# One order table for another: an attention-plus-gate kernel with its instruction order, engine choices, PSUM banks and filler matmuls replaced

## The chip, the cores and the metric

The kernel runs on one core of a Trainium2 chip. A core has five engines that run side by side and meet only through semaphores: TensorE (PE, matrix products into PSUM), VectorE (DVE), ScalarE (ACT), GpSimd (POOL) and SyncE (SP, which here only issues transfers). The metric is the device time of one execution in microseconds (us); less is better.

## The reference

Eight batches of eight heads, 576 rows, head size 64. Queries and keys pass through a feature map, the attention is linear, and its output goes into a gated linear unit with a causal convolution of five taps.

```python
def phi(x):
    proj = np.einsum('bhsd,df->bhsf', x, w_phi)              # f = 128
    proj = proj - np.max(np.abs(proj), axis=-1, keepdims=True)
    return np.concatenate([np.exp(proj), np.exp(-proj)], axis=-1)
q_p, k_p = phi(q), phi(k)
kv  = np.einsum('bhsf,bhsd->bhfd', k_p, v);  z = np.sum(k_p, axis=2)
num = np.einsum('bhsf,bhfd->bhsd', q_p, kv)
den = np.einsum('bhsf,bhf->bhs', q_p, z)[..., None] + 1e-06
x = (num / den)   # heads joined: [8, 576, 512]
gate = 1 / (1 + np.exp(-causal_conv5(x, conv_w)))            # per channel
return (gate * (x @ w_val)) @ w_out
```

## The kernel before

The work is cut into 1062 small tasks, and every task belongs to one engine (or to the transfer engines). `build` makes them in the same way in both kernels: for each of the eight batches, and for five units of up to four 128-column blocks each, it makes

- **loads**: batch 0's keys and queries come as float32 in nine pieces on SP's queue (`load32`, L525 and L527; four pieces of k, five of q) and are transposed on PE (`tp32`, L536) and copied to bf16 (`tc32`, L542 on DVE, L544 on ACT). From batch 1 on they are loaded and cast on POOL's queue (`load`, L550). Values come through `loadv` (L531): on POOL's queue for batch 1, on SP's for the others.
- **hold**: a one-column copy on POOL (`hold`, L509) that reads the last piece of batch 0's q. Since an engine works through its list in order, it keeps what stands behind it on POOL, the loads of batches 1 and 2, from being issued before that piece has landed.
- **keys**: projection on PE (`kp`, L577), maxima on DVE (`kmax`, L585), two exponentials per unit on ACT (`kexp`, L595), the row scale (`ek`, L604), v times that scale on POOL (`vs`, L610), and the product of keys and values (`st`, L620; its copy `kv`, L628/L632).
- **queries**: projection (`qm`, L577), maxima (`qmax`, L585), the maxima spread on POOL (`rx`, L682), projection less maxima (`qp`, L693/L698), exponentials (`qexp`, L706/L709).
- **output of the attention**: `num` (L719/L726), division on DVE (`nrm`, L737/L740), then the transpose into XT, on PE with a copy (`xtp`, `xtc`) or, in batches 6 and 7, by a transposing transfer issued from SP (`xtd`, L755).
- **gated unit**: `gate` (L781) with `tanh` (L785), `val` (L791) with `gv` (L797), `out` (L813, and L817 for the leftover rows of two batches), the copy out of PSUM (`oev`, L630 on DVE, L634 on ACT) and the store (`odma`, L830/L836).

Nothing schedules these at run time. `ORDER` is a table of task numbers: it is the order in which instructions are emitted, so each engine's list is the subsequence of its own tasks. `FLEX` says, for the 93 tasks that more than one engine can do, which engine does it (A, D or P). `BANKS` gives each group of tasks its PSUM bank or pair of banks. `WARM` and `ZERO` put extra matmuls on PE ahead of given places of the order: `warm` (L491) is one 512-column product whose result nobody reads, `zero` (L497/L504) adds zero products to a bank that a real task has just filled, so that whoever reads that bank waits for them too. Dependencies between engines become semaphore waits by themselves.

The loop that emits everything:

```python
for i, t in enumerate(plan.follow()):
    for _ in range(zero[i][1] if i in zero else 0):
        em.zero(plan.tasks[zero[i][0]])
    for _ in range(warm[i][1] if i in warm else 0):
        em.warm(warm[i][0])
    if t.fn is not None:
        t.fn(t)
```

## Time and profile before

| what | value |
|---|---|
| median of 3 runs | 219.54 us (218.94, 219.54, 221.03) |
| profiled execution, span from first to last instruction | 217.7 us |
| what lies around the span, by the median | 1.8 us |
| PE busy in the span | 195.5 us (90%), 3946 matmuls |
| ACT busy | 180.8 us (83%) |
| DVE busy | 170.2 us (78%) |
| POOL busy | 132.8 us (61%) |
| first exponential on ACT | at 9.21 us |
| last matmul over | at 212.52 us |

The profile gives the span of the one execution that it recorded and no whole time for it, so the median less the span stands for what lies around it. In the views quoted below, a row of the timeline begins with start and length in us, then engine and line, then what is written from what is read, and in brackets how long the engine stood idle ahead of it and who ended that. In a table of stretches the columns are length, busy time of PE, of its weight loads, of DVE, ACT and POOL (with the number of instructions), the granted PE clock, the share of the transfer engines and GB/s. A row of groups has its busy time, the mean duration in ns and the idle time ahead. A row of waits has the total, the number and the longest.

### The profile page before, as it was taken

Reading aid. Unit: us, or ns where it says so; the run is one execution under the profiler, and the core shown is the slowest. Engines: PE = TensorE matmul, PEld = TensorE weight load, DVE = VectorE, ACT = ScalarE, POOL = GpSimd, SP = SyncE. Lnnn points to the kernel's source line nnn. Section 1 sums busy time; section 2 is a strip of 40 time slices with the busy share of each in tenths; the row PEclk is TensorE's granted clock in tenths of the full one; section 3 lists DMA queues with packets and bytes.
Section 4 is the critical chain, followed back from the end, with each engine's and each line's share of the span. In section 5 each row is a group of like instructions: output and inputs, shape, how many; then the busy total and the mean of one; then the engine's idle time right before and its main releaser. Section 6 shows DMA issues by size and latency. Waiting matters only on the chain.

```text
span 217.7 us, 9029 instructions
## 1 busy us (share of the span) xinstructions
PE 195.5 (90%) x3946; PEld 138.6 (64%) x3946; DVE 170.2 (78%) x257; ACT 180.8 (83%) x267; POOL 132.8 (61%) x172
## 2 busy tenths in 40 slices
PE   2787887778999999998999999999999999899990
PEld 2555565566676676676857776567757766687740
DVE  3199979999789988997899978998699897654510
ACT  3589999999989899998999997999988988634251
POOL 3055999897793838970999089902993879210010
PEclk9999999999999999999999999999999999999997
DMA  6999998899899799989999778969953265764166
GB/s 177 364 234 215 302 188 231 149 174 199 144 152 284 139 135 213 302 154 174 233 276 168 88 165 248 190 142 203 287 183 89 63 160 128 81 168 97 48 186 202
DMA packets 49954, 39.92 MB, mean 183 GB/s; under 512 B 34165, under 2 KB 39541, under 8 KB 49914
## 3 DMA queue, kind: packets, MB, share of 16 engines
q1 hardware_dynamic: 43616, 28.65, 55.6%
q0 software_dynamic: 6032, 10.49, 26.3%
q8 instruction: 31, 0.51, 0.9%
q10 hardware_dynamic: 266, 0.21, 0.3%
q14 instruction: 9, 0.07, 0.1%
HBM read 30.48 MB, written 9.44 MB: 183 GB/s over the span
## 4 chain that ended last, share of the span: by engine, by line
PE 52%; ACT 23%; DVE 14%; DMA 5%; issue 4%; SPq 0%; DVEq 0%; ACTq 0%
PE PS L791 11%; ACT QTIL L706 9%; PE PS L781 9%; PE PS L813 9%; ACT KTIL L595 8%; DVE MQP L585 5%; PE PS L620 5%; PE PS L577 4%; PE PS L719 4%; DVE MK L585 3%; DMA KTIL<-in_k_dram 3%; PE PS L693 2%; DMA XT<-XN 2%; PE PS L817 2%; PE PS L698 2%
## 5 line engine op out<-in xcount | busy, mean ns | idle before, releaser
L595 ACT ACTIVATE KTIL<-PS 128x1024 bf16<-128x1024 f32 (+1 forms) x80 | 71.9, 960 | 4.1 <-PE PS L577 2.0
L610 POOL TENSOR_TENSOR VT<-VN,EK 128x1152 bf16<-128x1152 f32 x32 | 67.9, 2123 | 4.0 <-ACT EK L604 3.9
L706 ACT ACTIVATE QTIL<-PS 128x1024 bf16<-128x1024 f32 x64 | 62.5, 1044 | 2.4 <-PE PS L698 1.6
L682 POOL TENSOR_TENSOR RX<-MQR,ident 128x512 bf16<-128x512 bf16 (+1 forms) x39 | 36.6, 964 | 35.7 <-DVE MQR L670 26.0
L585 DVE TENSOR_REDUCE MK<-PS 128x8 f32<-128x1024 f32 (+1 forms) x40 | 44.2, 1112 | 2.9 <-PE PS L577 1.2
L585 DVE TENSOR_REDUCE MQP<-PS 128x8 bf16<-128x1024 f32 (+1 forms) x40 | 43.6, 1112 | 3.1 <-PE PS L577 2.3
L791 PE MATMUL PS<-XT,WV 128*128 128x288 bf16 x256 | 34.8, 286 | 0.3 <-DVE GV L797 0.2
L797 DVE SCALAR_TENSOR_TENSOR GV<-TH,PS 128x576 bf16<-128x576 bf16 x32 | 23.8, 752 | 10.4 <-PE PS L791 4.7
L813 PE MATMUL PS<-WOUT,GV 128*128 128x512 bf16 x128 | 31.3, 380 | 0.0
L791 PEld LDWEIGHTS <-WV 128*128 128x128 bf16 x256 | 23.8, 98 | 7.9 <-issue 1.4
L785 ACT ACTIVATE TH<-PS 128x576 bf16<-128x576 f32 x32 | 20.3, 663 | 9.5 <-PE PS L781 6.3
L620 PE MATMUL PS<-VT,KTIL 64*128 64x65 bf16 x1152 | 23.3, 191 | 1.1 <-issue 1.0
L781 PE MATMUL PS<-XT,GW 64*64 64x288 bf16 x640 | 23.1, 285 | 0.9 <-DMA XT<-XN 0.8
L740 DVE TENSOR_TENSOR XN<-PS,RCP 128x512 bf16<-128x512 f32 x32 | 22.1, 692 | 1.5 <-DMA XT<-XN 0.4
L620 PEld LDWEIGHTS <-KTIL 64*128 64x128 bf16 x1152 | 20.8, 94 | 3.8 <-issue 2.5
L719 PEld LDWEIGHTS <-QTIL 128*128 128x128 bf16 x512 | 18.3, 97 | 6.4 <-issue 4.0
L719 PE MATMUL PS<-KV,QTIL 128*128 128x65 bf16 x512 | 20.3, 194 | 0.3 <-DVE MQP L585 0.2
L781 PEld LDWEIGHTS <-GW 64*64 64x64 bf16 x640 | 17.8, 106 | 3.3 <-DVE RCP L737 0.9
L634 ACT ACTIVATE OUTS<-PS 128x512 f32<-128x512 f32 x22 | 13.5, 619 | 7.3 <-PE PS L813 6.1
L577 PE MATMUL PS<-W,qT 64*128 64x128 bf16 x288 | 15.1, 217 | 3.7 <-ACT qT L544 0.9
L813 PEld LDWEIGHTS <-GV 128*128 128x128 bf16 x128 | 11.1, 98 | 11.3 <-issue 0.6
L577 PEld LDWEIGHTS <-qT 64*128 64x128 bf16 x288 | 10.6, 94 | 10.3 <-issue 5.2
(79 smaller groups left out, 235.6 us busy)
## 6 DMA issues: line engine op xcount, KB each, us to landing
out_dram<-OUTS SPq DMA_DIRECT2D x32, 256.0 KB, 3.4
VN<-in_v_dram SPq DMA_DIRECT2D x7, 1152.0 KB, 6.3
KQN<-in_q_dram POOLq DMA_DIRECT2D x6, 576.0 KB, 8.3
KQN<-in_k_dram POOLq DMA_DIRECT2D x6, 576.0 KB, 9.8
KTIL<-in_k_dram SPq DMA_DIRECT2D x4, 288.0 KB, 4.5
VN<-in_v_dram POOLq DMA_DIRECT2D x1, 1152.0 KB, 10.6
KTIL<-in_q_dram SPq DMA_DIRECT2D x4, 256.0 KB, 5.7
out_dram<-OUTS SPq DMA_DIRECT2D x14, 64.0 KB, 2.6
```

The lines of the kernel that those rows point to most:

```text
L577: nc.tensor.matmul(self.PS[:, t.grp.banks[par], i * P:(i + 1) * P], X[rows, (c0 + i) * P:(c0 + i + 1) * P], self.W2[rows, :], start=True, ...
L585: self.nc.vector.tensor_reduce(o, self.two(t.grp, n * P).rearrange("p a (c f) -> p a c f", f=F), AX.X, ALU.max, apply_absolute_value=True)
L595: self.nc.scalar.activation(self.KTIL[b % 2][:, s, c0:c0 + n, :, :].rearrange("p c a f -> p a c f"), self.two(t.grp, n * P).rearrange("p a ...
L610: nc.gpsimd.tensor_tensor(self.VT[g][:, s, :, 0:D], self.VN[b % 2][:, NC * g:NC * g + NC, :], e.to_broadcast([P, NC, D]), ALU.mult)
L620: nc.tensor.matmul(self.PS[:, t.grp.banks[ab], (s * 2 + x) * E1:(s * 2 + x + 1) * E1], self.KTIL[b % 2][rows, s, J // 2, J % 2, :], self.V ...
L682: self.nc.gpsimd.tensor_tensor(o, *wide(self.MQR[self.mq(b, u)][:, :], self.ident2), ALU.mult)
L706: self.nc.scalar.activation(o, i, AF.Exp, scale=1.0 - 2.0 * s)
L719: nc.tensor.matmul(self.PS[:, t.grp.banks[h // 4], (h % 4) * E1:(h % 4 + 1) * E1], Q[:, s, c % 2, h, (c // 2) * P:(c // 2 + 1) * P], self. ...
L781: self.nc.tensor.matmul(self.PS[o * D:(o + 1) * D, t.grp.banks[par], 0:R], self.GW[r, jj, 4 - m, :], X[r, 4 * a + jj, :, HALO - 8 * s:HALO ...
L791: self.nc.tensor.matmul(self.PS[:, t.grp.banks[par], 0:R], self.WV[:, i, (2 * j + par) * D:(2 * j + par + 2) * D], X[:, 4 * par + i, :, HA ...
L797: nc.vector.scalar_tensor_tensor(out=self.GV[b % 3][:, j, :, :], in0=self.TH[j][:, :, :], scalar=1.0, in1=self.two(t.grp, R), op0=ALU.add, ...
L813: nc.tensor.matmul(self.PS[:, t.grp.banks[0], :], GV[:, j, c % 2, (c // 2) * XH:(c // 2) * XH + P], self.WOUT[:, j, c % 2, :], start=(j == ...
```

## The change

The functions are the same, line for line; five tables differ. The two tables at the top are shorter by two lines, so a line of the kernel before has a number smaller by 2 in the changed one (L595 becomes L593).

- `ORDER` holds the same 1062 tasks in another order. From about the 50th PE task on most tasks move by only a few places on their engine.
- `FLEX`: 21 tasks change engine. Twelve pass from ACT to DVE and eight from DVE to ACT; one spreading of maxima (`rx` of batch 0, unit 4) goes from DVE to POOL.
- `BANKS`: other PSUM banks for a number of groups.
- `ZERO`: 41 calls at 14 places become 10 calls at 3 places, 152 matmuls become 40. `WARM`: five places and six matmuls become four places and six matmuls.

```diff
-WARM = (
-    "60:6:1 81:1:1 87:7:2 134:7:1 141:7:1 "
-)
-ZERO = "35:76:7 61:80:5 75:34:1 101:105:1 118:99:1 126:215:8 144:223:1 155:192:4 158:200:1 175:315:6 189:346:1 195:241:2 197:241:2 211:327:1"
+WARM = "71:7:1 74:1:2 123:0:2 143:7:1"
+ZERO = "82:78:5 202:311:3 249:342:2"
...
-    "1 2 9 3 4 11 5 6 10 21 22 19 20 13 12 46 25 26 7 8 23 24 14 27 28 42 29 32 30 33 44 49 76 31 15 43 45 47 16 158 159 48 "
...
+    "1 2 3 4 27 28 7 8 21 22 19 20 5 9 6 25 182 26 23 24 40 11 183 29 10 158 41 159 160 42 12 161 301 44 46 302 32 47 45 30 "
...
-    "AAAAAADAAADDPPPPDDDDAADDDDDDDDDDDDDAAADAAAADDDDAAADDDAADAAADDADAADDDDADDDDADDDDDDAADADDAAAAAA"
+    "AAAADADAAADDPPPPPDDAAADDDDDDDDDDDDDDAADAADDDAADAAADDDAADADADDDDAADDDAADDADADADDADADADDDDADADD"
```

**The first loads, on SP.** KTIL1 here is the tile whose space first holds batch 0's float32 k and q, and VN0 holds values. SP's list began

```order
L527 DMA KTIL1_73<-in_k_dram 128x576 x3
L525 DMA KTIL1_73<-in_q_dram 128x512 x3
L527 DMA KTIL1_73<-in_k_dram 128x576
L525 DMA KTIL1_73<-in_q_dram 128x512
L525 DMA KTIL1_73<-in_q_dram 128x256
L531 DMA VN0_66<-in_v_dram 128x4x576
```

and now begins

```order
L525 DMA KTIL1_73<-in_k_dram 128x576 x2
L523 DMA KTIL1_73<-in_q_dram 128x256
L525 DMA KTIL1_73<-in_k_dram 128x576
L523 DMA KTIL1_73<-in_q_dram 128x512 x2
L525 DMA KTIL1_73<-in_k_dram 128x576
L523 DMA KTIL1_73<-in_q_dram 128x512 x2
L529 DMA VN0_66<-in_v_dram 128x4x576
```

The small last piece of q, the one that the hold reads, goes from ninth to third place, the third piece of k from third to seventh; the first full pieces of q come one place later.

**The first loads, on POOL.** After its memsets POOL's list went on with the hold, four loads (QTIL1 is batch 1's q and k, KQN are batch 2's), two spreadings of maxima (RX) and only then batch 1's values (VN1):

```order
L509 CAST HOLD_76<-KTIL1_73 128x1
L550 DMA QTIL1_75<-in_q_dram 128x2304
L550 DMA QTIL1_75<-in_k_dram 128x4x576
L550 DMA KQN1_65<-in_q_dram 128x2304
L550 DMA KQN0_64<-in_k_dram 128x4x576
L682 TENSOR_TENSOR RX1_135<-MQR0_90,ident2_130 128x512
L682 TENSOR_TENSOR RX0_134<-MQR0_90,ident2_130 128x512
L531 DMA VN1_67<-in_v_dram 128x4x576
L610 TENSOR_TENSOR VT0_82<-VN0_66,EK_86 128x18x64
```

and now

```order
L529 DMA VN1_67<-in_v_dram 128x4x576
L507 CAST HOLD_76<-KTIL1_73 128x1
L548 DMA QTIL1_75<-in_q_dram 128x2304
L548 DMA QTIL1_75<-in_k_dram 128x4x576
L548 DMA KQN1_65<-in_q_dram 128x2304
L680 TENSOR_TENSOR RX0_134<-MQR0_90,ident2_130 128x512
L680 TENSOR_TENSOR RX1_135<-MQR0_90,ident2_130 128x512
L457 DMA WV_139<-in_moe_w_val_dram 128x4x512
L548 DMA KQN0_64<-in_k_dram 128x4x576
L608 TENSOR_TENSOR VT0_82<-VN0_66,EK_86 128x18x64
```

Batch 1's values now stand ahead of the hold, batch 2's k stands behind the two spreadings, and the weights of `val` (WV) come right behind those spreadings, where they stood much further down.

**The first copies and exponentials, on ACT.** The casts are copies of transposed k (kT0) and q (qT0), the activations are exponentials of keys. Before:

```order
L544 CAST kT0_68<-PS_63 128x512 x3
L595 ACTIVATE KTIL0_72<-PS_63 128x2x4x128 x2
L544 CAST qT0_70<-PS_63 128x512
L595 ACTIVATE KTIL0_72<-PS_63 128x2x4x128
L544 CAST kT0_68<-PS_63 128x512
```

Now:

```order
L542 CAST kT0_68<-PS_63 128x512 x2
L593 ACTIVATE KTIL0_72<-PS_63 128x2x4x128 x3
L542 CAST qT0_70<-PS_63 128x512
L593 ACTIVATE KTIL0_72<-PS_63 128x2x4x128
L542 CAST kT0_68<-PS_63 128x512
```

The third copy of k leaves the head of the list, on PE the third transpose does the same, and the projections of the first two units follow the two transposes at once.

**The end.** On PE `num` of batch 6, chunk 0, stood behind two `st` of batch 7 and `qp` of batch 7's unit 2; it now follows `num` of chunk 1 directly, and those three tasks come after it. The last tasks on PE were seven `out` of batches 6 and 7 and, at the very end, the leftover rows (L817); now the leftover rows come fourth from the end and `out` of batch 7, chunk 0, is last.

10 lines of the change are left out of this document (5 added, 5 removed), and 70 rows, old and new, of the table ORDER.

## The prediction, on record before the changed kernel ran

> **What bounds the kernel now.** I read the page's busy shares first, then the table of stretches, then the timeline of the first 22 us and the chain that ended last. Shares and six of the stretches (length, busy PE, weight loads, DVE, ACT, POOL, then granted clock, transfer share, GB/s):
>
> ```profile
> PE 195.5 (90%) x3946; PEld 138.6 (64%) x3946; DVE 170.2 (78%) x257; ACT 180.8 (83%) x267; POOL 132.8 (61%) x172
> ...
> 0.00:10.00 10.00, 4.93 (x32) 3.83 (x33) 2.00 (x6) 3.83 (x5) 1.78 (x12) 1.00 0.82 258
> 10.00:20.00 10.00, 7.73 (x122) 5.60 (x121) 9.32 (x10) 9.34 (x15) 5.68 (x8) 1.00 1.08 244
> 40.00:50.00 10.00, 7.38 (x202) 5.88 (x197) 8.94 (x16) 9.78 (x13) 9.97 (x10) 1.00 0.96 166
> 100.00:110.00 10.00, 9.98 (x210) 7.55 (x200) 9.25 (x18) 8.31 (x15) 6.93 (x9) 1.00 1.08 216
> 160.00:170.00 10.00, 10.00 (x200) 7.04 (x199) 9.15 (x12) 9.03 (x15) 5.20 (x8) 1.00 0.26 74
> 210.00:217.70 7.70, 2.52 (x16) 0.86 (x13) 0.00 (x0) 2.24 (x4) 0.00 (x0) 0.85 0.70 220
> ```
>
> Three regimes are to be seen. Up to 10 us almost nothing works. From 10 to about 55 us ACT is full (9.3 to 9.8 of ten) and PE is not (7.4 to 7.7). Later PE is full. So a reordering of the full middle, whose work stays the same, can give little; the gain or loss must come from how early ACT's stream begins, from how well inputs keep up with it, and from the last 30 us. An earlier start reaches the end only if PE then turns full earlier as well.
>
> **The start.** The timeline up to 22 us, and two rows of stretches for the transfers:
>
> ```profile
> 3.85 2.23 PE L536 MATMUL PS<-ident_f,KTIL 128*128 128x128 f32 x9 [3.85 <-DMA KTIL<-in_k_dram]
> 4.97 0.59 ACT L544 CAST kT<-PS 128x512 bf16<-128x512 f32 x1 [0.93 <-PE PS L536]
> 5.29 0.23 DVE L455 CAST W<-W 128x128 bf16<-128x128 f32 x1 [2.48 <-DMA W<-in_w_phi_dram]
> 5.91 0.59 ACT L544 CAST kT<-PS 128x512 bf16<-128x512 f32 x1 [0.35 <-PE PS L536]
> 7.29 0.90 PE L536 MATMUL PS<-ident_f,KTIL 128*128 128x128 f32 x3 [1.21 <-DMA KTIL<-in_k_dram]
> 8.13 1.04 PE L577 MATMUL PS<-W,kT 64*128 64x128 bf16 x16
> 9.10 1.78 PE L536 MATMUL PS<-ident_f,KTIL 128*128 128x128 f32 x8
> 9.21 1.94 ACT L595 ACTIVATE KTIL<-PS 128x1024 bf16<-128x1024 f32 x2 [0.39 <-PE PS L577]
> 11.01 0.19 POOL L509 CAST HOLD<-KTIL 128x1 bf16<-128x1 f32 x1 [8.62 <-DMA KTIL<-in_q_dram]
> 11.07 0.40 PE L577 MATMUL PS<-W,qT 64*128 64x128 bf16 x8 [0.19 <-DVE qT L542]
> 21.87 2.11 POOL L610 TENSOR_TENSOR VT<-VN,EK 128x1152 bf16<-128x1152 f32 x1 [2.09 <-ACT EK L604]
> ```
>
> ```profile
> 3.40:7.00 3.60, 2.23 (x9) 1.64 (x9) 0.23 (x1) 1.82 (x3) 0.00 (x0) 1.00 1.01 292
> 7.00:10.50 3.50, 3.21 (x26) 2.68 (x27) 0.18 (x1) 1.88 (x3) 0.00 (x0) 1.00 1.02 372
> ```
>
> PE had done two transposes by about 5.9 us (eight of the nine matmuls that start at 3.85 and take 2.23) and then stood for 1.21 us in the third, whose piece of k had not landed. Everything for the first projection was there: ACT had copied the first unit by 4.97 + 0.59 = 5.56, DVE had cast the weights by 5.52. But projections came behind that third transpose, from 8.13, and the first exponential began at 9.21.
>
> In the new order PE goes straight to the projections. From 5.9 they take half of 1.04, so about 0.5; ACT ends its second copy at 6.50 and can begin the exponentials at about 6.7, **2.5 us earlier** than 9.21. On DVE the maxima follow in the same way. That is the largest term, and it is worth what the next inputs leave of it. ACT's list now holds three exponentials (each half of 1.94, so 0.97) before the first copy of q: it is busy until about 9.6. In the kernel before, q's first two pieces were transposed from 9.10 on, eight matmuls with no wait on a transfer, so they had landed by about 10, having been fourth and fifth on SP; now they are fifth and sixth.
>
> **What speaks against it** is POOL. The hold waited 8.62 us, and so SP's first pieces had the transfer engines to themselves, at 292 and 372 GB/s. Now batch 1's values (1152 KB) stand ahead of the hold and start when POOL's memsets are over (nearly all of its 1.78 us in the first ten), at some 2 to 3 us; and the hold reads a piece that is third in the queue, so the loads of batches 1 and 2 follow early too.
>
> ```profile
> VN<-in_v_dram POOLq DMA_DIRECT2D x1, 1152.0 KB, 10.6
> ```
>
> The bounds of that cost: nothing, if the pieces land before they are due; and 1152 KB / 292 GB/s = 4.0 us, if all of the values went first. No row of before has both queues loading at the start. Sharing evenly over the 7 us until the last pieces are due would take some 2 us from pieces that have about 1.5 us to spare; I charge 0.7. So the start brings 2.5 - 0.7 = **1.8 us**, with ends of +1.5 (loss) and -2.5. DVE, POOL and PE are not what stops it: POOL's first product waited 2.09 us for ACT's row scale (the row at 21.87), and that row scale now stands six places earlier on ACT.
>
> The Trainium skill has a rule for the shared part: "DMA: Bandwidth & Descriptors", section on queues, rings and completion order, says each transfer engine takes turns between the queues that have work. By it SP would keep about half of the rate, the pieces would come about 2 us later, and the start would bring about 1 us. No run here shows the two at once yet.
>
> **The filler matmuls.** 112 of 152 zero products go. Their rows, and who waited for them in the first 60 us:
>
> ```profile
> 11.98 0.96 PE L504 MATMUL PS<-ONES,NIL 64*128 64x128 bf16 x28
> 13.25 0.40 PE L577 MATMUL PS<-W,qT 64*128 64x128 bf16 x8 [0.31 <-ACT KTIL L595]
> ...
> PE PS L504 <- ACT QTIL L706: 1.1, 1, 1.1
> ACT QTIL L706 <- PE PS L504: 0.6, 2, 0.4
> DVE MQP L585 <- PE PS L504: 0.5, 2, 0.3
> ```
>
> At 0.96 / 28 = 34 ns each the 112 cost 3.8 us of PE, nearly all of it in stretches where PE had nothing else, so removing it gives no PE time on the path. What it gives is the readers' waits, of which the 0.6 on ACT count; since ACT would then wait for the real product, which lies just ahead, I take **0.3** (ends 0 and 0.6). The cover for PE time is ACT's full stream; if that were gone, the 3.8 would come off PE.
>
> **The middle.** By the table of engine choices ACT gives away more copies than it takes:
>
> ```profile
> L634 ACT ACTIVATE OUTS<-PS 128x512 f32<-128x512 f32 x22 | 13.5, 619 | 7.3 <-PE PS L813 6.1 <-PE PS L817 0.9 <-DMA out_dram<-OUTS 0.3
> L632 ACT COPY XT<-PS 128x1024 bf16<-128x1024 bf16 x2 | 2.1, 1043 | 0.0
> ```
>
> Up to batch 5 its balance is one output (0.62) and two large XT copies (2 x 1.04) given away, one KV given and one taken, and two small XT copies (a quarter of the large ones' size) taken: about 2.7 us less, before the small ones. PE is full there, so I count **0** of it (ends 0 and -2.7).
>
> **The last 30 us.** The chain that ended last:
>
> ```profile
> 181.93 0.68 PE PS L620 x36
> 184.05 0.61 PE PS L719 x16
> 185.71 4.54 DMA XT<-XN
> ```
>
> ```profile
> 190.38 2.03 PE L781 MATMUL PS<-XT,GW 64*64 64x288 bf16 x60 [0.77 <-DMA XT<-XN]
> 211.47 1.05 PE L817 MATMUL PS<-WOUT,GVT 128*64 128x512 bf16 x8
> 212.61 0.60 ACT L634 ACTIVATE OUTS<-PS 128x512 f32<-128x512 f32 x1 [0.44 <-PE PS L817]
> 213.24 1.48 ACTq L836 DMA_DIRECT2D out_dram<-OUTS  x2
> ...
> out_dram<-OUTS SPq DMA_DIRECT2D x32, 256.0 KB, 3.4
> out_dram<-OUTS ACTq DMA_DIRECT2D x2, 64.0 KB, 2.9
> ```
>
> PE waited 0.77 us for a transposing transfer, because `num` (184.05) stood behind two `st` (0.68 each) and a `qp`. Those come after it now, so the transfer starts over a microsecond earlier and the wait closes; SP has three stores between its two transposes now, which eats a part: **0.5** (ends 0 and 0.77). At the very end, two small transfers were issued in sequence (1.48 us, the second landing 2.9 after its issue at about 213.98, so 3.6 after 213.24); now one of 256 KB is last, landing 3.4 after issue: **0.2** (ends +0.5, if it queues behind the store before it, and -0.5).
>
> **Sum.** 1.8 + 0.3 + 0 + 0.5 + 0.2 = 2.8 us off the span of 217.7, so 214.9; with the 1.8 that lies around it 216.7, against a median of 219.54.
>
> **The rivals.** (1) *The start does not arrive.* ACT begins early but POOL, DVE or a late transpose of batch 1 gives it back by 55 us. For it: POOL at 9.97 and ACT at 9.78 in 40 to 50, so two engines must both move up. Against it: POOL was held by the row at 21.87. Only the end's 0.7 would stay: 218.8. (2) *Contention at the start.* The early values take all they could: pieces of q, and the third of k, 4.0 us late. ACT has only the 2.5 us of its early start to live on, so it loses 1.5; less the end's 0.7 that is 220.3. It decides once the lateness passes 2.5. Against it: rates rose from 292 to 372, so there was room. (3) *The clock falls* without the fillers. The granted clock fell in this run only in the last stretch (0.85), with PE done at 212.52. What a slower PE would cost: early, eight projections took 1.04 / 2 = 0.52 against 0.40 at 11.07; 0.12 for each of the 75 PE tasks that the order table has up to 55 us is 9 us if all were on the path. Half of that, 4.5, with 1.3 of the 1.8 gone, gives 222.5. Against it: the longest PE gap without its filler is that at 11.98, 0.96 + 0.31 = 1.3 us, and a gap of 1.1 (ahead of a filler) was borne before.
>
> The Trainium skill speaks for this one: "TensorE: Matmul & The Clock Gate", on a second failure mode, tells of a kernel whose short idles between groups of products made the clock swing. By it rival 3 happens; the trace shows short idles and no fall, but with fillers in place.
>
> (4) *More than the sum*: ACT's idle time from 10 to 55 us closes too, 0.66 and 0.22 in the two stretches shown, some 2 us over the whole: 214.7.
>
> **How the numbers follow.** Forecast 0.47 (its own range 215.3 to 218.0), rival 1 0.22, rival 2 0.14, rival 3 0.08, rival 4 0.09. The predicted time is 216.7. About 1% (2.2 us) is what a measurement of this kernel tells from no change. Faster by more than that means below 217.3: nearly three quarters of the forecast (0.35), all of rival 4 (0.09), and a little of rival 1 (0.06): 0.50. Slower needs over 221.7: rival 3 with 0.07 and the far end of rival 2 with 0.03: 0.10. The rest is 0.40. The range leaves out most of rival 3 and the best part of rival 4: 213.9 to 221.0.
>
> **What would show it.** Right: the first exponential near 6.7 us; the first product of POOL well before 21.87; ACT over 9 in every stretch from 10; PE's wait for the transfer near 190 gone; clock 1.00 everywhere but at the end. Wrong: idle time on PE, DVE or ACT ahead of q's first copies ended by a transfer (rival 2); a clock under 1.00 between 10 and 55 us (rival 3); an early first exponential with PE no fuller before 55 us (rival 1).

## The result and the profile after

| | kernel before | changed kernel |
|---|---|---|
| median | 219.89 us (4 runs, 218.94 to 221.03) | 238.39 us (4 runs, 236.51 to 239.38) |
| ratio, 95% interval | | 1.0875 (1.0787 to 1.0962) |
| profiled execution | | 239.38 us, span 237.6 us |

The changed kernel is slower by 8.7%, where 1.3% less was forecast. The medians and ratios of the sections below leave out the executions that took over 1.5% more than the fastest of the same kernel. The page of the changed kernel (busy time and share of the span; then the granted clock of PE in 40 slices of 5.9 us, in tenths):

```profile
PE 200.3 (84%) x3815; PEld 140.8 (59%) x3834; DVE 173.0 (73%) x260; ACT 179.3 (75%) x263; POOL 133.9 (56%) x173
PEclk9999999859999988999999997999979999999999
```

ACT and POOL work as long as before within 1.5 us, DVE 2.8 us and PE 4.8 us longer. The span is 19.9 us longer: most of the time went into waiting. The clock, which was full up to the last stretch before, falls in four places.

Stretches of the changed kernel (the columns are those explained ahead of the prediction):

```profile
0.00:10.00 10.00, 3.18 (x24) 2.21 (x24) 2.82 (x7) 5.31 (x6) 4.81 (x17) 1.00 0.80 272
10.00:20.00 10.00, 6.97 (x46) 4.86 (x47) 4.70 (x5) 3.50 (x5) 0.00 (x0) 1.00 1.10 282
40.00:50.00 10.00, 6.84 (x156) 5.24 (x156) 8.75 (x11) 10.00 (x14) 9.11 (x11) 0.80 0.75 172
160.00:170.00 10.00, 8.28 (x176) 5.82 (x174) 7.50 (x14) 9.01 (x14) 4.74 (x5) 1.00 1.07 247
```

In the second stretch ACT worked 3.50 us where it had worked 9.34, DVE 4.70 where 9.32. In 160 to 170, where PE was full, it now stands for 1.7 us, and the transfer engines are busier (1.07 against 0.26). The 1.00 of the first two stretches hides something: a stretch without a record of the clock counts as 1.00, and the first record in the trace comes at 22.11 us, where it came at 10.55 in the kernel before. Up to then eight projections took 0.61 us, afterwards 0.40. In the run with the values back, below, it comes at 8.26. So the early waits also kept PE slow for some 11 us longer.

**The start.** Its timeline, PE, then ACT, then POOL:

```profile
6.21 1.14 PE L575 MATMUL PS<-W,kT 64*128 64x128 bf16 x16
10.63 1.12 PE L534 MATMUL PS<-ident_f,KTIL 128*128 128x128 f32 x4 [3.29 <-DMA KTIL<-in_q_dram]
13.32 1.12 PE L534 MATMUL PS<-ident_f,KTIL 128*128 128x128 f32 x4 [1.57 <-DMA KTIL<-in_q_dram]
15.80 1.12 PE L534 MATMUL PS<-ident_f,KTIL 128*128 128x128 f32 x4 [0.83 <-DMA KTIL<-in_k_dram]
...
6.85 2.85 ACT L593 ACTIVATE KTIL<-PS 128x1024 bf16<-128x1024 f32 x3 [0.17 <-PE PS L575]
14.47 0.59 ACT L542 CAST qT<-PS 128x512 bf16<-128x512 f32 x1 [4.76 <-PE PS L534]
...
2.50 0.94 POOL L529 DMA_DIRECT2D VN<-in_v_dram  x1
6.55 0.56 POOL L548 DMA_DIRECT2D QTIL<-in_q_dram  x1
20.61 2.04 POOL L680 TENSOR_TENSOR RX<-MQR,ident 128x512 bf16<-128x512 bf16 x2 [12.21 <-DVE MQR L665]
```

The projections and the first exponential (6.85) came early, as forecast. Then PE stands for 3.29, 1.57 and 0.83 us ahead of transposes whose pieces of q and k have not landed, and ACT for 4.76 us. The table of transfers names the reason; the last number is the median time from issue to landing in us:

```profile
VN<-in_v_dram POOLq DMA_DIRECT2D x1, 1152.0 KB, 9.1
KTIL<-in_q_dram SPq DMA_DIRECT2D x4, 256.0 KB, 10.3
```

The full pieces of q needed 10.3 us; in the kernel before it was 5.7:

```profile
KTIL<-in_q_dram SPq DMA_DIRECT2D x4, 256.0 KB, 5.7
```

Counted from the packets that start in each microsecond of the trace, POOL's queue (batch 1's values first) and SP's queue (the urgent pieces) moved, in KB per us:

| us | POOL's queue | SP's queue | SP's in the kernel before |
|---|---|---|---|
| 6 to 7 | 272 | 99 | 326 |
| 7 to 8 | 364 | 38 | 331 |
| 8 to 9 | 258 | 76 | 372 |

**Later.** Three waits, each with what was issued ahead of it. First near 85 us (SP, then PE), then near 141 (POOL, SP, PE), then near 171:

```profile
77.89 0.55 SPq L529 DMA_DIRECT2D VN<-in_v_dram  x1
79.29 5.36 SPq L563 DMA_TRANSPOSE kT<-KQN  x1
87.40 0.74 PE L618 MATMUL PS<-VT,KTIL 64*128 64x65 bf16 x20 [2.37 <-issue]
...
121.66 0.61 POOL L548 DMA_DIRECT2D KQN<-in_q_dram  x1
122.42 0.53 SPq L529 DMA_DIRECT2D VN<-in_v_dram  x1
122.72 0.75 POOL L548 DMA_DIRECT2D KQN<-in_k_dram  x1
135.50 2.73 SPq L563 DMA_TRANSPOSE kT<-KQN  x1
141.25 0.29 PE L575 MATMUL PS<-W,kT 64*128 64x128 bf16 x4 [2.56 <-DMA kT<-KQN]
...
161.00 0.51 SPq L529 DMA_DIRECT2D VN<-in_v_dram  x1
161.62 6.01 SPq L563 DMA_TRANSPOSE qT<-KQN  x1
171.30 0.29 PE L575 MATMUL PS<-W,qT 64*128 64x128 bf16 x4 [2.75 <-DMA qT<-KQN]
```

Each time a load of 1152 KB of values (VN) is issued just ahead of, or among, the transfers that PE needs next (`issue` in the first says that the profile names nothing that PE waited for). In the kernel before the values came behind both transfers, as here for batch 7:

```profile
143.95 2.71 SPq L565 DMA_TRANSPOSE kT<-KQN  x1
146.76 2.69 SPq L565 DMA_TRANSPOSE qT<-KQN  x1
154.09 0.91 SPq L531 DMA_DIRECT2D VN<-in_v_dram  x1
```

Behind each wait the clock falls. Stretches ahead of a fall and in it:

```profile
80.00:87.00 7.00, 4.78 (x164) 3.57 (x161) 4.49 (x5) 6.41 (x9) 1.96 (x2) 1.00 1.12 229
87.00:90.40 3.40, 2.78 (x68) 2.36 (x69) 1.90 (x3) 0.42 (x1) 1.73 (x2) 0.50 1.18 255
...
135.00:141.50 6.50, 3.94 (x100) 3.11 (x96) 2.95 (x6) 4.19 (x8) 5.75 (x6) 1.00 0.97 132
141.50:145.00 3.50, 3.50 (x18) 1.79 (x13) 1.39 (x2) 3.02 (x4) 1.63 (x3) 0.51 0.95 206
```

Behind each of these three waits of 2.4 to 2.8 us the clock is at 0.50 for 3.4 us, so here a wait costs more than its length. That is no rule: with both repairs, below, PE stood for 3.21 us at this first place and no fall followed. The granted clock in these traces changes only in steps of about 3.41 us, so PE's idle time in each step can be read. In the 17 traces with records of the clock, all 27 falls ahead of the last products came behind steps with 1.33 to 2.89 us of idle time, and every step with more than 1.82 us was followed by a fall. The 3.21 us lay across two steps, with 1.82 and 1.38 us in them. So in these traces it is partly chance, by where a wait lies on the steps, whether it also costs clock. The remaining fall, from 46 us on, has no transfer ahead of it: ACT is full there (10.00 of ten) and PE stands in small pieces.

How late a product runs can be read by finding the same task in two traces. The table gives the start of some PE tasks in the profiled executions (unit 0 or chunk 0 of the batch, where there are several), the kernel before in us, the others as the difference to it (minus is earlier). The experiments below use the same rows; their names are those of the sections.

| task (batch) | before | changed | V1 back | late loads | both | + batch 3 | + batch 5 |
|---|---|---|---|---|---|---|---|
| projection of keys, unit 0 (0) | 8.53 | -2.3 | -2.7 | -2.7 | -2.8 | -2.6 | -2.5 |
| output product, chunk 0 (0) | 69.67 | +5.8 | -2.4 | +3.7 | -1.7 | -1.7 | -1.1 |
| first key projection (4) | 84.62 | +9.8 | +1.8 | +5.8 | +1.9 | -1.6 | -0.9 |
| `num`, chunk 0 (4) | 123.41 | +9.9 | +2.0 | +8.6 | +2.0 | -0.1 | -0.5 |
| `st` (5) | 135.43 | +14.2 | +6.1 | +8.6 | +2.0 | -0.1 | -0.5 |
| output product, chunk 0 (4) | 169.97 | +19.0 | +9.3 | +8.8 | +2.2 | +0.1 | -0.3 |
| end of the span | 217.67 | +19.9 | +10.1 | +9.6 | +3.0 | +0.9 | +0.5 |

Read downwards, the changed kernel loses in four steps: about 8.2 us between the projection of unit 0 and 70 us, 4.0 near 85, 4.2 near 140, 4.8 near 171 us. (The very first projection, which is unit 1's in the kernel before, came at 8.13 there and at 6.21 here, 1.9 us earlier.)

### The profile page after: what moved, and what is told of

Read it like the earlier page. It is cut to its first block, busy times and chain, and to the rows that moved or that the text cites. A ratio compares the mean times of both kernels' runs of the same rounds, so it can differ in the third digit from the quotient of the medians.

```text
span 237.6 us, 8786 instructions
## 1 busy us (share of the span) xinstructions
PE 200.3 (84%) x3815; PEld 140.8 (59%) x3834; DVE 173.0 (73%) x260; ACT 179.3 (75%) x263; POOL 133.9 (56%) x173
## 4 chain that ended last, share of the span: by engine, by line
PE 52%; DMA 15%; DVE 12%; ACT 12%; issue 5%; SPq 1%; DVEq 0%; ACTq 0%
PE PS L789 12%; PE PS L811 9%; PE PS L779 7%; ACT KTIL L593 6%; ACT QTIL L704 5%; PE PS L575 5%; DMA KTIL<-in_k_dram 5%; PE PS L618 4%; DVE MQP L583 4%; PE PS L717 4%; DMA qT<-KQN 4%; DVE MK L583 3%; PE PS L691 3%; DMA kT<-KQN 2%; DMA XT<-XN 2%
## 5 line engine op out<-in xcount | busy, mean ns | idle before, releaser
L593 ACT ACTIVATE KTIL<-PS 128x1024 bf16<-128x1024 f32 (+1 forms) x80 | 71.9, 944 | 8.3 <-DVE MK L583 3.8
L704 ACT ACTIVATE QTIL<-PS 128x1024 bf16<-128x1024 f32 x64 | 63.4, 1034 | 6.4 <-PE PS L696 5.9
L680 POOL TENSOR_TENSOR RX<-MQR,ident 128x512 bf16<-128x512 bf16 (+1 forms) x40 | 37.3, 956 | 44.2 <-DVE MQR L668 20.5
L789 PE MATMUL PS<-XT,WV 128*128 128x288 bf16 x256 | 37.9, 302 | 0.2 <-DVE GV L795 0.2
L789 PEld LDWEIGHTS <-WV 128*128 128x128 bf16 x256 | 25.0, 103 | 10.1 <-issue 1.9
L811 PE MATMUL PS<-WOUT,GV 128*128 128x512 bf16 x111 | 29.5, 382 | 1.1 <-issue 0.4
L783 ACT ACTIVATE TH<-PS 128x576 bf16<-128x576 f32 x32 | 19.9, 659 | 9.9 <-PE PS L779 6.1
L717 PEld LDWEIGHTS <-QTIL 128*128 128x128 bf16 x512 | 19.0, 100 | 6.3 <-issue 4.7
L575 PE MATMUL PS<-W,kT 64*128 64x128 bf16 x288 | 16.1, 230 | 6.9 <-DMA kT<-KQN 2.6
L717 PE MATMUL PS<-KV,QTIL 128*128 128x65 bf16 x512 | 21.0, 198 | 0.7 <-DVE MK L583 0.7
L632 ACT ACTIVATE OUTS<-PS 128x512 f32<-128x512 f32 x18 | 10.9, 607 | 11.2 <-PE PS L811 10.6
L575 PEld LDWEIGHTS <-kT 64*128 64x128 bf16 x288 | 10.5, 100 | 13.2 <-issue 7.8
## 6 DMA issues: line engine op xcount, KB each, us to landing
KTIL<-in_q_dram SPq DMA_DIRECT2D x4, 256.0 KB, 10.3
```

Source lines behind the costliest of these rows:

```text
L575: nc.tensor.matmul(self.PS[:, t.grp.banks[par], i * P:(i + 1) * P], X[rows, (c0 + i) * P:(c0 + i + 1) * P], self.W2[rows, :], start=True, ...
L593: self.nc.scalar.activation(self.KTIL[b % 2][:, s, c0:c0 + n, :, :].rearrange("p c a f -> p a c f"), self.two(t.grp, n * P).rearrange("p a ...
L680: self.nc.gpsimd.tensor_tensor(o, *wide(self.MQR[self.mq(b, u)][:, :], self.ident2), ALU.mult)
L704: self.nc.scalar.activation(o, i, AF.Exp, scale=1.0 - 2.0 * s)
L717: nc.tensor.matmul(self.PS[:, t.grp.banks[h // 4], (h % 4) * E1:(h % 4 + 1) * E1], Q[:, s, c % 2, h, (c // 2) * P:(c // 2 + 1) * P], self. ...
L789: self.nc.tensor.matmul(self.PS[:, t.grp.banks[par], 0:R], self.WV[:, i, (2 * j + par) * D:(2 * j + par + 2) * D], X[:, 4 * par + i, :, HA ...
```

## The experiments

**Theory A**: the new order issues bulk loads ahead of urgent transfers, at the start and in three places later; PE waits, and the clock falls because it waited. **Rival B**: at the start it is the early hold, not the values. **Rival C**: the clock falls because the fillers are gone, and that is the loss. **Rival D**: the queues share without harm, as the prediction had it. Edits to the order table are shown as the engine's list of instructions. Each verdict is a ratio to the kernel before on the same chip, whose median was 218.5 to 219.0 us in these runs.

### Batch 1's values back behind the loads (V1 back)

```diff
 POOL of the changed kernel
-L529 DMA VN_67<-in_v_dram 128x4x576
 L507 CAST HOLD<-KTIL_73 128x1
...
 L548 DMA KQN_64<-in_k_dram 128x4x576
+L529 DMA VN_67<-in_v_dram 128x4x576
 L608 TENSOR_TENSOR VT_82<-VN_66,EK 128x18x64
```

> The changed kernel with one POOL entry put back: batch 1's values are issued behind the hold, the four loads and the two spreadings, as before; SP's list and every other list stay as changed. Theory A (bulk loads get ahead of urgent ones): the values took most of the transfer rate from 3 to 12 us, so the first q pieces land some 3 to 5 us earlier, the gate products of batch 0 come 2 to 5 us earlier than in the changed kernel (59.0 there), and the end follows: 233 to 236.5 us. The clock falls at 87, 142 and 172 us stay, each moved earlier by the same amount. Rival B (the early hold, not the values, starves SP: 576 KB loads simply take the place of the values): within 1 us of the changed kernel's 238.4. Rival C (the missing fillers let the clock fall, and the start is not what counts): also within 1 us of 238.4, with the first q pieces on time all the same.

231.50 us, 1.0561 (1.0475 to 1.0647), 6.9 below the changed kernel and a little below the expected 233 to 236.5. The transfers and ACT at the start:

```profile
KTIL<-in_q_dram SPq DMA_DIRECT2D x4, 256.0 KB, 4.6
```

```profile
6.52 3.03 ACT L593 ACTIVATE KTIL<-PS 128x1024 bf16<-128x1024 f32 x3
9.45 0.58 ACT L542 CAST qT<-PS 128x512 bf16<-128x512 f32 x1
```

The pieces of q land in 4.6 us, ACT goes from its three exponentials straight to q, and the output product of batch 0, chunk 0, starts 2.4 us ahead of the kernel before, where it was 5.8 behind. Rival B falls: the hold is still early here, and the lead of 2.4 us is there. The later steps stay (4.2, 4.1 and 3.2 us in the table), the last of them without a fall of the clock.

### The late loads of batches 6 and 7 (late loads)

```diff
 POOL of the changed kernel
+L548 DMA KQN_65<-in_q_dram 128x2304
+L548 DMA KQN_64<-in_k_dram 128x4x576
 L608 TENSOR_TENSOR VT_83<-VN_66,EK 128x18x64
...
-L548 DMA KQN_65<-in_q_dram 128x2304
 L766 COPY XT_101<-XT_101 128x16x2x7
 L767 COPY XT_101<-XT_101 128x8x2
-L548 DMA KQN_64<-in_k_dram 128x4x576
 SP
 L563 DMA_TRANSPOSE kT_69<-KQN_64 128x18x128
+L563 DMA_TRANSPOSE qT_71<-KQN_65 128x18x128
 L529 DMA VN_67<-in_v_dram 128x4x576
-L563 DMA_TRANSPOSE qT_71<-KQN_65 128x18x128
```

> The changed kernel with two entries moved and nothing at the start: on POOL the q and k loads of batch 6 go ahead of the two products of values with row scale (2.2 us each) and the halo copy; on SP the 1152 KB load of batch 7's values goes behind the transposing transfer of batch 7's q. Theory A: the two waits of PE (2.56 us to 141.25, 2.75 us to 171.30) and the two clock falls behind them (3.4 us each) go, so the lag steps of 4.2 and 4.5 us go: 228.5 to 231.5 us. Theory A with rebound (the transfers come earlier but the next transfer, stores or the last transposes, takes the wait over): 232 to 236. Rival C (the clock falls for want of fillers whatever the loads do): falls of the granted clock to 0.5 stay near 140 and 170 us, and the time stays above 236.

229.29 us, 1.0452 (1.0380 to 1.0524), 9.1 below the changed kernel; the two steps of 4.2 and 4.8 in the table are gone, while 2.8 us are lost between 90 and 123 us, where PE now waits twice for POOL (1.13 and 1.68 us). SP near batch 7's transfers, and the clock:

```profile
153.76 2.69 SPq L563 DMA_TRANSPOSE kT<-KQN  x1
156.59 3.39 SPq L563 DMA_TRANSPOSE qT<-KQN  x1
160.08 0.53 SPq L529 DMA_DIRECT2D VN<-in_v_dram  x1
```

```profile
PEclk9999999999999999999999999999999999999997
```

With 40 fillers instead of 152, and nothing mended but these loads, the clock does not fall before the end of this execution; the mean clocks of two others, 0.948 and 0.981, say that it did fall there. So the late falls near 141 and 172 us need the waits, and few fillers alone do not bring them, which speaks against rival C.

### The values first, in the kernel before

```diff
 POOL of the kernel before
+L531 DMA VN_67<-in_v_dram 128x4x576
 L509 CAST HOLD_76<-KTIL1_73 128x1
...
-L531 DMA VN_67<-in_v_dram 128x4x576
 L610 TENSOR_TENSOR VT0_82<-VN_66,EK 128x18x64
```

> The kernel before with one entry of the change alone: batch 1's values are issued on POOL ahead of the hold, right behind the memsets. Theory A: they take most of the rate up to about 9 us, so the first k and q pieces land 2 to 4 us later, the first exponential comes at 10 to 13 us where it was 9.21, and the end is 2 to 5 us later: 222 to 225 us. Rival D (the two queues share and there was room, as the prediction had it: 0.7 us lost): 219 to 221. If the early order of the exponentials is what made the values harmful, the same as D.

222.27 us, 1.0162 (1.0096 to 1.0227). PE at the start:

```profile
9.96 0.65 PE L536 MATMUL PS<-ident_f,KTIL 128*128 128x128 f32 x4 [1.45 <-DMA KTIL<-in_q_dram]
12.64 0.90 PE L536 MATMUL PS<-ident_f,KTIL 128*128 128x128 f32 x3 [1.43 <-DMA KTIL<-in_k_dram]
```

The entry alone costs 3.6 us, with two waits of 1.4 us that the kernel before did not have. The time is as expected, a detail is not: the first exponential came at 7.82, not later than 9.21, because the third piece of k was there in time in this execution. The clock was at 0.50 from 11.5 to 21.7 us here, but that does not seem to be what costs: two executions with a mean clock of 0.996 and 1.000 took 221.61 and 223.06 us. In the changed order the same entry costs more (6.9), where the hold is early too and 576 KB loads follow the values; that this is the reason was not tried.

### The kernel before without fillers

```diff
-ZERO = "35:76:7 61:80:5 75:34:1 101:105:1 118:99:1 126:215:8 144:223:1 155:192:4 158:200:1 175:315:6 189:346:1 195:241:2 197:241:2 211:327:1"
+ZERO = ""
```

> The kernel before with all 152 zero products left out and nothing else changed (the 6 warming matmuls stay; the output is the same). Rival C (without fillers the clock falls): a granted clock under 1.00 somewhere between 10 and 210 us and a time of 222 us or more. Theory A: the longest PE gap becomes 1.3 us, no fall of the clock, and the time is 218.5 to 220.5 us, 0 to 0.6 less than before from the readers' waits.

220.38 us, 1.0072 (1.0033 to 1.0111). Clock, and stretches that end where it falls:

```profile
PEclk9985999997899999999999999999999999999997
```

```profile
12.20:15.60 3.40, 2.07 (x30) 1.47 (x30) 3.38 (x4) 3.40 (x6) 1.67 (x3) 0.93 1.01 209
49.60:53.00 3.40, 1.94 (x35) 1.50 (x36) 1.80 (x5) 1.98 (x3) 1.05 (x5) 0.95 1.11 165
```

In the kernel before rival C has a point: two falls, each behind a stretch of 3.40 us of which PE worked 2.07 and 1.94, and some 1.6 us lost. That the falls make the loss was not shown. No single wait there was over 1.33 us. It is small beside 19, but it has the other sign than the forecast's term for the fillers.

### Both repairs (both), and batch 3's values (+ batch 3)

The first kernel has the two repairs of the changed kernel together. The second also moves one SP entry:

```diff
 SP of the changed kernel, batch 3 then 4
 L563 DMA_TRANSPOSE qT_71<-KQN_65 128x18x128
+L529 DMA VN_67<-in_v_dram 128x4x576
 L828 DMA out_dram<-OUTS_111 16x8x512
-L529 DMA VN_67<-in_v_dram 128x4x576
 L563 DMA_TRANSPOSE kT_68<-KQN_64 128x18x128
```

> The changed kernel with the two repairs together: batch 1's values behind the hold and the early loads on POOL, batch 6's loads ahead of two products on POOL, batch 7's values behind the transposing transfer of q on SP. Theory A, adding up the lags of the two single runs (start 2.4 us ahead of the kernel before, 4.1 us lost at the stall near 77 us with its clock fall, about 1 us lost in the last 40): 2.7 us above the kernel before, some 221.3 us (219 to 223.5), with no fall of the clock near 134 and 163 us. Rival (the gains don't add, since a kernel that runs earlier meets its transfers later): 224 to 228.

221.08 us from two executions, 1.0109 (0.9998 to 1.0221), against 221.3 expected; by lags too the gains add (3.0 at the end against 2.7 expected). The place that is near 85 us in the changed kernel, and that these two repairs do not touch, on SP and PE:

```profile
72.09 6.37 SPq L563 DMA_TRANSPOSE kT<-KQN  x1
80.74 0.50 PE L618 MATMUL PS<-VT,KTIL 64*128 64x65 bf16 x20 [3.21 <-issue]
```

> As the run with the two repairs, and on SP the 1152 KB load of batch 3's values goes up behind batch 3's transposing transfers, as in the kernel before; in the changed kernel it is issued right ahead of batch 4's transposing transfers, while PE stands for 2.3 us without a wait that the profile names. Theory A (the values' load slows the transposing transfers and PE's instruction fetch): the first transposing transfer of batch 4 takes near 3.3 us on SP where it took 5.4, PE's stall shrinks below 1 us, the clock does not fall there, and the end comes 3 to 4 us earlier than in the run with the two repairs: 216.5 to 218.5 us. Rival (the stall is instruction supply alone and has nothing to do with that load): the stall of over 2 us stays and the time is within 1 us of the run with the two repairs.

220.32 us, 1.0083 (1.0049 to 1.0118), above the expected 216.5 to 218.5. SP now, with batch 4's transposing transfers undisturbed:

```profile
73.29 3.24 SPq L563 DMA_TRANSPOSE kT<-KQN  x1
77.00 3.32 SPq L563 DMA_TRANSPOSE qT<-KQN  x1
```

The first transfer takes 3.24 us on SP, where it took 5.36 in the changed kernel and 6.37 with both repairs, and PE's stall there (2.37 and 3.21 us) is gone. In the profiled executions this is worth 3.5 us at batch 4 and 2.1 at the end; by the medians it is 0.8 us, and the intervals overlap, so what this load costs in time is not settled. Why the load stood there is seen in the diff: a store of batch 0's output, new ahead of it, made SP wait for that output.

### Fillers put back

All 41 calls of the kernel before, behind the same products, first in the kernel with three repairs, then in the changed kernel alone:

```diff
-ZERO = "82:78:5 202:311:3 249:342:2"
+ZERO = "47:76:7 64:34:1 73:80:5 82:78:5 107:105:1 122:99:1 132:215:8 145:223:1 160:200:1 161:192:4 179:315:6 188:346:1 193:241:2 194:241:2 202:311:3 213:327:1 249:342:2"
```

> As the run with all three repairs, and the 41 calls of fillers of the kernel before (152 zero products) are put back behind the same products, beside the 40 that the changed kernel has. Rival C (fillers hold the clock up): the granted clock stays 1.00 up to 210 us, and the time is 1 to 3 us below the run with the three repairs. Theory A: once the loads are in order PE has no idle stretch long enough, so the fillers do nothing or cost up to 2 us of PE time: -0.5 to +2 us.

222.98 us, 1.0193 (1.0118 to 1.0267): some 2.6 worse than without, where theory A allowed 2. The clock is now full up to the last slice, the same row as with the late loads repaired, as rival C said; but the time is not lower for it.

> The changed kernel with the 152 zero products of the kernel before put back and every load left as the change has it. Rival C (the missing fillers are the cause of the loss): the clock falls go and the time is 222 to 230 us. Theory A (late transfers are): the falls behind the waits near 87, 141 and 172 us stay, at most the one near 46 us goes, and the time is 235 to 240 us.

238.64 us, 1.0912 (1.0850 to 1.0974), the changed kernel's 238.39 again, with falls at 86 and 144 us. The falls at 46 and 172 us are gone and the time is the same. Rival C is out as a cause of this change's loss.

### Batch 5's values (+ batch 5)

```diff
 SP of the kernel with three repairs, batch 5 then 6
 L563 DMA_TRANSPOSE qT_71<-KQN_65 128x18x128
+L529 DMA VN_67<-in_v_dram 128x4x576
 L828 DMA out_dram<-OUTS_115 16x8x512
 L834 DMA out_dram<-OUTS_111 16x2x512 x4
-L529 DMA VN_67<-in_v_dram 128x4x576
```

> As the run with three repairs (values of batch 1 back, loads of batches 6 and 7 in order, values of batch 3 early), and on SP the 1152 KB load of batch 5's values goes up behind batch 5's transposing transfers, as it were in the kernel before: in the run with three repairs it was issued at 111.96, the transposing transfer of batch 6's k then took 5.12 us on SP and PE stood 1.09 us with no wait named; lag there went from -1.2 to -0.1. Theory A: that transfer takes near 3 us, PE's stall goes, and the end comes 1.0 to 1.6 us earlier than the run with three repairs: 218.3 to 219.5 us by its median of 220.36. Rival: no change, 220 to 221.

221.02 us, 1.0126 (1.0053 to 1.0198). The transfer that took 5.12 us on SP now:

```profile
119.05 2.69 SPq L563 DMA_TRANSPOSE kT<-KQN  x1
121.85 3.65 SPq L563 DMA_TRANSPOSE qT<-KQN  x1
```

The stall of 1.09 us is gone as expected, but the time is not lower, so the expected 218.3 to 219.5 was missed. Other small waits differ between executions by as much.

### Which part of the step near 140 us

The edit of the section before, alone in the changed kernel:

> The changed kernel with one SP entry moved: the 1152 KB load of batch 5's values goes up behind batch 5's transposing transfers; batch 6's loads stay late on POOL. If the wait of 2.56 us near 141 comes from the values sharing the transfer engines with the two loads of batch 6 (issued at 121.66, 122.42 and 122.73 in the changed kernel): the transposing transfer of batch 6's k starts 2 us or more earlier against its neighbours, the step of 4.2 us in the lag shrinks below 2, and the time is 234 to 236.5 us. If the late issue of the loads on POOL alone does it: the step stays, 237.5 to 239.

233.82 us, 1.0680 (1.0604 to 1.0755), 4.6 below the changed kernel; the lag between `num` (4) and `st` (5) does not grow any more. Issue of the two loads on POOL, then SP's next transposing transfer:

```profile
118.35 0.61 POOL L548 DMA_DIRECT2D KQN<-in_q_dram  x1
119.41 0.75 POOL L548 DMA_DIRECT2D KQN<-in_k_dram  x1
129.52 3.32 SPq L563 DMA_TRANSPOSE kT<-KQN  x1
```

From the second load to the transfer that needs it: 10.1 us, where it was 12.8 (122.72 to 135.50) with the values in between.

And the kernel with four repairs, with batch 6's loads taken back to their late place:

```diff
 POOL
-L548 DMA KQN_65<-in_q_dram 128x2304
-L548 DMA KQN_64<-in_k_dram 128x4x576
 L608 TENSOR_TENSOR VT_83<-VN_66,EK 128x18x64
...
+L548 DMA KQN_65<-in_q_dram 128x2304
 L766 COPY XT_101<-XT_101 128x16x2x7
 L767 COPY XT_101<-XT_101 128x8x2
+L548 DMA KQN_64<-in_k_dram 128x4x576
```

> As the run with four repairs, with one of them taken back: batch 6's loads stand on POOL behind the two products of 2.2 us and the halo copy, as the change has them (batch 5's values early, batch 7's values late). If the late issue is a cause by itself: 1.5 to 4 us over the run with four repairs, 222.5 to 225, with a wait of PE for batch 6's k. If it hurts only together with batch 5's values: 220 to 222, as the run with four repairs; the kernel before with the same entry showed no step there, with batch 5's values early.

220.64 us, 1.0092 (1.0050 to 1.0133), as with four repairs (221.02). PE does wait 1.04 us for batch 6's k here, but the time does not show it. So the late place on POOL alone costs nothing measurable; it hurts together with the values. My first reading, that the two products on POOL ahead of the loads were the cause, was wrong.

This kernel is also the plainest answer to the whole question: it is the changed kernel with four loads of values moved (batches 1, 3, 5 and 7) and nothing else, and it takes 220.64 us where the changed kernel takes 238.39.

### Three entries of the change in the kernel before

```diff
 POOL of the kernel before: batch 1's values first, as above, and
-L550 DMA KQN_65<-in_q_dram 128x2304
-L550 DMA KQN_64<-in_k_dram 128x4x576
 L610 TENSOR_TENSOR VT_83<-VN_66,EK 128x18x64
 L611 CAST VT_83<-EK 128x18
 L610 TENSOR_TENSOR VT_82<-VN_66,EK 128x18x64
 L611 CAST VT_82<-EK 128x18
+L550 DMA KQN_65<-in_q_dram 128x2304
+L550 DMA KQN_64<-in_k_dram 128x4x576
 SP
 L565 DMA_TRANSPOSE kT_69<-KQN_64 128x18x128
+L531 DMA VN_67<-in_v_dram 128x4x576
 L565 DMA_TRANSPOSE qT_71<-KQN_65 128x18x128
...
-L531 DMA VN_67<-in_v_dram 128x4x576
```

> The kernel before with three entries of the change and nothing else: batch 1's values first on POOL, batch 6's loads on POOL behind two of the 2.2 us products, batch 7's values on SP between the two transposing transfers of batch 7. Fillers, PE, ACT and DVE lists, banks and engine choices as before. Theory A (these entries suffice): 3.6 + about 4 + about 4 us over the kernel before, 228 to 232.5 us, with PE waits of over 2 us for both transposing transfers and a clock fall behind each. Rival (they hurt only in the new order of PE and without fillers): 221.5 to 225 us.

228.71 us, 1.0469 (1.0402 to 1.0536). SP and PE at batch 7:

```profile
151.59 0.53 SPq L531 DMA_DIRECT2D VN<-in_v_dram  x1
152.23 6.03 SPq L565 DMA_TRANSPOSE qT<-KQN  x1
161.88 0.40 PE L577 MATMUL PS<-W,qT 64*128 64x128 bf16 x4 [3.53 <-DMA qT<-KQN]
```

Against the kernel before PE is 4.2 us late from 70 us on, with no step at batch 6, and 9.2 from batch 7 on: the values first and the values between the two transfers do it, with all fillers in place and PE's order untouched. The step expected for batch 6 did not come, which led to the two runs above.

### The end, the start, and some fillers

Five kernels asked where the early start's 2.5 us went, the first three made from the kernel with four repairs. The small output last, as in the kernel before:

```diff
 last products of PE, all of batch 7
-out 2, out 4 (small), out 3, out 1, out 0
+out 2, out 3, out 1, out 0, out 4 (small)
```

> As the run with four repairs, and the last lines of the order are as in the kernel before: the product, copy and stores of the small leftover output (64 KB pieces on SP and ACT) come last, behind the 256 KB one. The time from the end of the last product to the end of the span was 5.2 us in the kernel before and 5.6 to 5.7 with the large store last. Theory: 0.3 to 0.6 us less than the run with four repairs, 217.8 to 219.0, so no measurable gain over the kernel before. Rival (the large store last is no worse, the difference is chance): within 0.2 us of the run with four repairs.

220.13 us, 1.0082 (1.0043 to 1.0122), beside 1.0126 (1.0053 to 1.0198) with the large store last: the intervals overlap, not settled.

SP's first loads in the old order:

```diff
 SP
-L525 DMA KTIL_73<-in_k_dram 128x576 x2
+L525 DMA KTIL_73<-in_k_dram 128x576 x3
+L523 DMA KTIL_73<-in_q_dram 128x512 x3
+L525 DMA KTIL_73<-in_k_dram 128x576
+L523 DMA KTIL_73<-in_q_dram 128x512
 L523 DMA KTIL_73<-in_q_dram 128x256
-L525 DMA KTIL_73<-in_k_dram 128x576
-L523 DMA KTIL_73<-in_q_dram 128x512 x2
-L525 DMA KTIL_73<-in_k_dram 128x576
-L523 DMA KTIL_73<-in_q_dram 128x512 x2
```

> As the run with four repairs, and SP's nine first loads in the order of the kernel before (third piece of k third, the small piece of q that the hold reads last), PE, ACT and DVE in the changed order. It tests the start term by itself (2.5 us earlier start, through to the end). If the gain at the start hangs on the new load order: 1 to 2.5 us more than the run with four repairs, 219.5 to 222. If PE's order alone brings it: within 0.7 us of it.

222.77 us, 1.0192 (1.0142 to 1.0242): some 1.8 us worse than with the new order of loads, though the intervals just overlap. The lead at the projection of unit 0 is the same (2.7 us), and is smaller by 30 us (0.9 against 1.5 at batch 1's first key projection), with a fall of the clock from 19.4 to 26.2 us (19.7 to 23.1 with the new order of loads).

Fillers only between 25 and 45 us:

```diff
-ZERO = "82:78:5 202:311:3 249:342:2"
+ZERO = "82:78:5 107:105:1 122:99:1 132:215:8 145:223:1 160:200:1 161:192:4 202:311:3 249:342:2"
```

> As the run with four repairs, and of the fillers of the kernel before only those that stand between about 25 and 45 us are put back (16 of 41 calls), not those of the first 20 us, which delayed PE by 2.2 us there. In the run with four repairs the clock fell from 40.2 to 43.6 us behind a stretch with 2.5 us of PE idle time in five waits on ACT and DVE, and the lead over the kernel before shrank from 1.7 to 1.2 us. If that fall is what the missing fillers cost: no fall near 40 us, the lead stays, and the median comes 0.5 to 1.5 us lower, 219.3 to 220.5. Rival (ACT sets the pace there, PE's clock does not matter, fillers delay the readers): within 0.4 us, or up to 1 us more.

222.69 us, 1.0201 (1.0146 to 1.0255): some 1.6 us worse than without (1.0126) with intervals that overlap, and not better. Whether the fall near 40 us was gone cannot be read, since the profiled execution of this kernel is of no use (see the end); holding the clock there did not pay, in any case.

The changed order for the first 75 tasks, in the kernel before, and its companion with only the three early places of fillers left out. The companion's edit, which both have, and the first tasks of the order table:

```diff
-ZERO = "35:76:7 61:80:5 75:34:1 101:105:1
+ZERO = "101:105:1
-    "1 2 9 3 4 11 5 6 10 21 22 19 20 13 12 46 25 26 7 8 23 24 14 27 28 42 29 32 30 33 44 49 76 31 15 43 45 47 16 158 159 48 "
+    "1 2 3 4 27 28 7 8 21 22 19 20 5 9 6 25 26 23 24 40 11 29 10 158 41 159 160 42 12 161 301 44 46 302 32 47 45 30 33 49 "
...
```

> The kernel before with the changed order for its first 75 tasks alone (loads, first transposes, projections, copies and exponentials of batch 0; batch 1's values not among them, they stay behind the spreadings), its own banks and engine choices, and without the three early calls of fillers (13 of 41 calls), which delayed PE by 2.2 us when they stood in the changed start. All that follows is as before. The prediction's start term, undisturbed: the first exponential near 6.6 us, and a lead of 1.8 to 2.5 us that stays to the end since the rest is the kernel before: 216.3 to 217.2 us against 218.8. Rival (the lead is given back by the queues and readers that follow in the first 60 us): 218 to 219.5.

225.36 us, 1.0295 (1.0250 to 1.0339). The projection of unit 0 was 2.5 us ahead, and by batch 1's first key projection PE was 2.8 us behind, with a clock fall from 19.1 to 26.0 us. Part of that may be the fillers left out, which the companion has out too.

> The kernel before without its first three calls' places of fillers (13 of 41 calls, standing at 10 to 22 us) and nothing else: the companion of the run with the changed start. If those fillers only hold the clock: a fall near 15 to 22 us as in the run without any, and 0.3 to 1.5 us more than before, 219 to 220.3. If they are idle work: 218.3 to 219.

222.66 us, 1.0174 (1.0124 to 1.0223): those 13 calls are worth about 3.7 us, more than all 41 together (1.6). This I cannot explain. Against this companion the changed start loses another 1.2% (1.0295 against 1.0174, the intervals apart), some 2.7 us: without those fillers the early start brings no gain in the kernel before. What it would bring with the early fillers in place was not tried.

No version beat the kernel before.

## Why the prediction was wrong

**The first exponential 2.5 us earlier: right.** It came at 6.85 instead of 9.21, 2.4 us earlier, for the reason given, and without the early values the lead is still 2.4 us at 70 us. That this lead reaches the end as a gain is not borne out: no repaired kernel has it there.

**"I charge 0.7" for the shared start: the step that failed first.** The values cost about 8.2 us of lag at 70 us, and 6.9 by the median. The values were issued at 2.50 us, as foreseen, and their first packets ran from 5.57 us on. The upper bound, 4.0 us, was also too low, because it took the values as the only competitor: the pieces of q landed 4.6 us later (10.3 against 5.7), the loads behind the hold followed at 6.55, POOL's first spreading waited 12.21 us, and eight projections of PE still took 0.61 us at 18 us, where they take 0.40 at the full clock. Rival 2 named the mechanism, and its own condition (lateness over 2.5 us) was met; its price, 1.5 us, was the lateness less the lead, as if the rest of the chain had no further use for the transfers. The Trainium skill, "DMA: Bandwidth & Descriptors", section on queues, rings and completion order, has each transfer engine take turns between queues with work; the trace does not agree with the half that I made of it: SP's queue got 99 of 371 KB in one microsecond and 38 of 402 in the next. Counted in packets of data, which are twice as large on POOL's queue, it was 47 beside 59 and then 18 beside 79, so equal turns fit the first microsecond roughly and the second not.

**The middle "0": the step that failed by most.** I weighed the balance of ACT and DVE and the fullness of PE, and did not look at where in SP's and POOL's lists the later loads stood. Three loads of 1152 KB had moved to just ahead of, or among, the transfers that feed batches 4, 6 and 7: a step of 4.0 us in the trace for the first (by the medians not settled), and 9.1 us by the median for batches 6 and 7 together; the second of these loads alone, put back, gave 4.6. With the early values of batch 1 the four loads make 17.8 us (238.39 to 220.64). A full PE is no shelter: in the table the lag of the changed kernel grows from step to step and never shrinks again. In the balance itself I counted one output too many for ACT: up to batch 5 it gives two away and takes two, which changes nothing in a term of 0.

**Fillers -0.3: wrong sign in the kernel before, nothing in the changed one.** Taking all away there costs some 1.6 us (1.0072), with clock falls that I had excluded because no single gap passed 1.3 us; the falls came behind stretches with 1.3 to 1.5 us of idle time in several pieces. The Trainium skill's rule on short idles ("TensorE: Matmul & The Clock Gate", second failure mode) holds here. But putting the fillers into the changed kernel left it at 238.64, so rival 3 was rightly held unlikely as the cause; three of the four falls stand right behind the late waits.

**The last 30 us -0.7: wrong.** With the loads repaired the lag grows by 0.8 us between batch 4's output product and the end (+0.1 to +0.9, and -0.3 to +0.5). PE's wait for the transposing transfer, 0.77 us before, was 0.59 in the run with the late loads repaired: it did not close. Which part is the order on PE and which the large last store was not settled.

**What stays open.** With four repairs the kernel is still 1.3% slower (1.0126), and the lead of 2.5 us at the projection of unit 0 is all but gone by 170 us. It goes in small pieces that differ between executions. The changed banks and engine choices were not tried alone; with the order of the products and the fillers they share the 1 to 3 us that are left when only the four loads are moved (1.0050 to 1.0133). How the fillers' worth depends on their place is not understood either.

## What to carry to other kernels

When an order changes, list the position of every large load in its queue against the small urgent transfers near it, along the whole kernel and not only at the start: here four loads of 1152 KB out of place made some 18 us, while everything else in the five tables together made 1 to 3. Price such a load by what it delays and by what waits behind that, not by its own bytes divided by the rate. A clock fall in a profile is first to be read as the trace of waits just ahead of it.

## What was not expected of the hardware

- Two queues with work did not share evenly: POOL's values, in packets of 4608 bytes, got 258 to 364 KB per us, SP's pieces, in packets of 2048 and 2304 bytes, 38 to 99.
- The clock fell to 0.50 for 3.4 us (or two or three times that) behind idle times of 1.3 to 2.9 us within a step of 3.4 us; no idle time of 3.4 us was needed, and 3.21 us across two steps brought no fall.
- PE stood for 2.37 us with no wait named, while a values load and transposing transfers ran; with the load moved away the stall went. That its instructions came late by the same transfer engines is not shown. With both repairs it fits: an instruction packet of 16 KB at 76.5 us took 2.8 us, where others took 0.9 to 1.5, and PE stood for 3.21 us from 77.5 us. In the changed kernel the packet ahead of the stall took 1.1 us, and a stall of 1.01 us near 120 us stands in the last kernel of the step near 140 us too, with batch 5's values early.
- In the runs with some fillers and without three calls the profiled execution took 623.84 and 365.2 us, PE's products being slow from end to end; the other executions of the same kernels took 221.8 to 224.2 and 221.4 to 224.1. Those two traces are not used here, and their cause is unknown.
